# Seven block products instead of eight for batch 1's second expert layer, in a fused kernel on one Trainium2 core

## The chip, the cores and the metric

The kernel runs on one core of one Trainium2 chip. The metric is the device time of one execution in microseconds. Before the change it is 1129.08 us, the median of three runs (1128.8 to 1129.44).

## What is computed

Three stages follow each other on 2304 tokens (4 batches of 576, here columns) with 512 features. An attention over 32 memory slots gives `x`; a layer pair `x @ w_in` (512 to 2048), leaky ReLU, `@ w_out` follows; the last stage, where the change lies, mixes four experts:

```python
def _moe2_ref(x, domain_probs, w1, w2):          # x 2304x512, w1 4x512x1024, w2 4x1024x512
    p = domain_probs / (domain_probs.sum(-1, keepdims=True) + 1e-09)
    out = np.zeros((N, D), dtype=np.float32)
    for e in range(E):
        h = np.maximum(x @ w1[e], 0.0)
        out += p[:, e:e + 1] * (h @ w2[e])
    return out.astype(np.float32)
```

## The kernel before

Every float32 operand of a large product is split into a high part (a cast on ScalarE) and a low part (the difference, on VectorE or GpSimd). A product of two 128x128 by 128x288 blocks is then three matmuls: high by high, high by low, low by high (`PASSES`).

The experts' 4 x 1024 hidden features are cut into eight groups `g` of 512, and each group into two halves `hp` of 256. A *unit* is one group for one batch. The plan of `plan_experts` (L1110) runs in two halves: in the first, units (g, 0) and (g, 1) for g = 0 to 7, in the second (g, 2) and (g, 3). Within a unit, class `Up` makes the first product by Strassen's algorithm: seven block products `p1` to `p7` per half, 6 matmuls each, into three PSUM tiles (`ux`, `uy`, `uw`), from which `v1`, `v16`, `v167`, `c11`, `c22`, `c21`, `c12` form the four blocks of `h`; a gate then takes the maximum with zero and multiplies by `p`. The second product of a unit runs beside the first product of the next one, in the places that `down()` leaves.

There are two forms of the second product. Class `Down` (L981), for batches 0 and 1 and for group 7, makes 8 products of 12 matmuls (L1000), from the gated `h` split into `g` tiles. Class `Seven` (L1024), for batches 2 and 3 in groups 0 to 6, uses Strassen's algorithm: differences of gated blocks (`sum`, L1040), high and low parts into `gc` tiles, 14 products of 6 matmuls (L1060), evacuated into seven accumulators per batch (`flush`, L1075), which `combine` turns into the output at the end. Its weights are four blocks of `w2` and four operand sums `S1` to `S4`, made in the first half by `s_sum` (GpSimd), `s_part` and `s_keep`, stored in DRAM and loaded in the second half.

```python
self.seven, self.hs = b > 1 and g < NG - 1, None                     # Up, L888 on
def c11(self):
    nc.scalar.copy(out=self.block(0, 0), in_=self.x)
def c22(self):
    self.add(self.block(1, 1), self.w, self.v167_t)
def gate(self, i):
    h = self.h[:, 2 * i:2 * i + 2].rearrange("p j n -> p (j n)")
    nc.vector.scalar_tensor_tensor(out=h, in0=h, scalar=0.0, in1=p_t[self.g // 2, self.b], op0=ALU.max, op1=ALU.mult)
```

PSUM holds six banks for `ux`, `uy`, `uw` (`ps_a`) and two for the second product (`ps_h`). The pool `big` has ten buffers; in the first half seven hold the operands `x` of batches 0 and 1, and the `g` tiles share the rest. Every engine takes its instructions in order. That order is the list `ORDER` (L30) of task names, such as `p1_300` (product 1 of group 3, batch 0, half 0), `D21_3` and `F21_3` (product 3 of group 2, batch 1, and its evacuation), `H`/`L` (high, low part), `S` (difference); `ON_VECTOR` (L254) says which low parts and differences go to VectorE and not to GpSimd. Before the change the list keeps one regular order, that of the plan, from group 2 of the first half to group 4 of the second; before and behind these (groups 0 and 1, the layer pair of the second stage, and the last groups) it is irregular. The change makes it irregular from group 0 of the first half to group 1 of the second, and regular from there to group 6.

## Time and profile before

| what | value |
|---|---|
| median of three runs | 1129.08 us |
| profiled execution: its time, its span | 1128.83 us, 1126.7 us |
| TensorE busy, matmuls | 1117.2 us, 8752 |
| VectorE, ScalarE, GpSimd busy | 797.8, 440.8, 529.7 us |
| DMA moved | 181.21 MB |

The span is the time between the first and the last instruction; 2.1 us of the execution lie around it. Busy times count an engine's instructions, overlaps once; in the profile PE is TensorE's matmuls, PEld its weight loads, DVE VectorE, ACT ScalarE, POOL GpSimd, SP the queue that issues the transfers. `L1000` is a line of the kernel. A tile's name stands left of the arrow, what it is made from right of it. A matmul's duration holds the time in which the next one already runs.

### The profile page before, as it was taken

To read this page: it belongs to the slowest core of one execution; us is meant where nothing else is said; L and a number is where in the kernel's file an instruction comes from. 1 tells how busy PE (TensorE), PEld (TensorE's weight loads), DVE (VectorE), ACT (ScalarE), POOL (GpSimd) and SP (SyncE) were. 2 spreads that over 40 slices of the span, in tenths; PEclk is the share of its full clock that TensorE was granted. 3 is DMA by queue.
4 is the path that set the end of the run, shared out by engine and by line. 5 is a ranking of instruction groups with operands and counts; after the bars stand their busy time and mean duration, and the time that the engine had idled before them with its cause. 6 is when DMAs were issued, how large, how long until landed. Compare 5 with 4: busy or idle time off the path is not lost.

```text
span 1126.7 us, 22094 instructions
## 1 busy us (share of the span) xinstructions
PE 1117.2 (99%) x8752; PEld 1082.7 (96%) x8752; DVE 797.8 (71%) x1469; ACT 440.8 (39%) x916; POOL 529.7 (47%) x432
## 2 busy tenths in 40 slices
PE   9999999999999999999999999999999999999998
PEld 7679999999999999999999999999999999999998
DVE  6987787667556766576676767687577777777776
ACT  5776655544444444233333323333432222222220
POOL 3666545523346567474554745433333333334650
PEclk9999999999999999999999999999999999999999
DMA  9930212111021449373653637675556455555432
GB/s 378 394 124 20 94 57 76 57 39 40 1 86 42 152 156 355 114 293 142 241 224 132 260 147 269 233 260 183 161 180 186 160 181 159 176 163 169 134 109 87
DMA packets 64503, 181.21 MB, mean 161 GB/s; under 512 B 6672, under 2 KB 23056, under 8 KB 60688
## 3 DMA queue, kind: packets, MB, share of 16 engines
...
## 4 chain that ended last, share of the span: by engine, by line
PE 95%; DVE 2%; POOL 1%; issue 1%; DMA 0%; ACT 0%; POOLq 0%; DVEq 0%; ACTq 0%
PE o L1000 19%; PE y L688 17%; PE c L1060 13%; PE uy L887 13%; PE h L654 9%; PE uw L887 8%; PE ux L887 8%; PE y L685 1%; PE pw L613 1%; PE warm L320 1%; PE pm L422 1%; PE h L651 1%; PE pc L454 0%; POOL w L307 0%; DMA raww<-in_w 0%
## 5 line engine op out<-in xcount | busy, mean ns | idle before, releaser
L1000 PE MATMUL o<-g,w 128*128 128x288 f32 x1536 | 223.3, 295 | 1.6 <-ACT acc L1015 1.6
L1000 PEld LDWEIGHTS o<-g,w 128*128 128x128 f32 x1536 | 210.0, 188 | 1.8 <-ACT acc L1015 1.8
L688 PE MATMUL y<-g,wout 128*128 128x288 f32 x1440 | 205.3, 296 | 0.0
L688 PEld LDWEIGHTS y<-g,wout 128*128 128x128 f32 x1440 | 195.3, 188 | 7.3 <-ACT g L673 2.5
L887 PE MATMUL uy<-x,w 128*128 128x288 f32 x1152 | 184.7, 296 | 0.4 <-DVE v L921 0.4
L887 PEld LDWEIGHTS uy<-x,w 128*128 128x128 f32 x1152 | 163.1, 188 | 1.9 <-DVE v L921 1.7
L1060 PE MATMUL c<-gc,w2c 128*128 128x288 f32 x1008 | 155.9, 295 | 0.5 <-ACT acc L1073 0.5
L1060 PEld LDWEIGHTS c<-gc,w2c 128*128 128x128 f32 x1008 | 140.9, 188 | 1.0 <-ACT acc L1073 1.0
L307 POOL TENSOR_TENSOR gc<-h,gc 128x576 fp32r<-128x576 f32 x54 | 81.5, 1517 | 124.9 <-ACT gc L1047 91.5
L307 POOL TENSOR_TENSOR g<-act,g 128x288 fp32r<-128x288 f32 x78 | 67.6, 873 | 121.1 <-ACT g L673 86.3
L887 PE MATMUL uw<-x,w 128*128 128x288 f32 x768 | 122.6, 295 | 0.0
L887 PE MATMUL ux<-x,w 128*128 128x288 f32 x768 | 122.1, 295 | 0.0
L654 PE MATMUL h<-a,wp 128*128 128x288 f32 x720 | 110.2, 296 | 0.0
L887 PEld LDWEIGHTS uw<-x,w 128*128 128x128 f32 x768 | 108.8, 188 | 0.1
L887 PEld LDWEIGHTS ux<-x,w 128*128 128x128 f32 x768 | 108.8, 188 | 0.0
L669 DVE SCALAR_TENSOR_TENSOR act<-neg,bet,h 128x288 f32<-128x288 f32 x120 | 60.2, 509 | 65.2 <-ACT neg L660 59.4
L654 PEld LDWEIGHTS h<-a,wp 128*128 128x128 f32 x720 | 100.0, 188 | 5.7 <-issue 2.3
L1047 ACT CAST gc<-h 128x576 fp32r<-128x576 f32 x70 | 47.1, 675 | 146.2 <-DVE h L1040 114.8
L1017 DVE TENSOR_TENSOR acc<-o,acc 128x288 f32<-128x288 f32 x112 | 50.7, 453 | 69.5 <-PE o L1000 69.5
L307 POOL TENSOR_TENSOR w<-raww,w 128x512 fp32r<-128x512 f32 (+1 forms) x45 | 69.1, 1551 | 62.4 <-ACT w L791 38.9
L921 DVE TENSOR_TENSOR v<-uy,v 128x288 f32<-128x288 f32 x128 | 58.1, 454 | 48.5 <-PE uy L887 45.6
L660 ACT ACTIVATE neg<-h 128x288 f32<-128x288 f32 x128 | 52.2, 411 | 97.4 <-PE h L654 94.9
(175 smaller groups left out, 1627.3 us busy)
## 6 DMA issues: line engine op xcount, KB each, us to landing
...
```

The lines of the kernel that those rows point to most:

```text
L307: eng.tensor_tensor(out=out, in0=in0, in1=in1.bitcast(F32), op=ALU.subtract)
L320: mm(p[:, 0:128], ident, ident, start=True, stop=True)
L654: mm(p, wp_t[b, c, g][:, x, fs], a_t[b][:, y, g, o:o + HB], start=(n == 0), stop=(n == 5))
L660: nc.scalar.activation(out=self.neg, in_=self.p, func=AF.Relu, scale=-1.0)
L669: nc.vector.scalar_tensor_tensor(out=self.g, in0=self.neg, scalar=bet[:, ft:ft + 1], in1=self.p, op0=ALU.mult, op1=ALU.add)
L688: mm(First.acc[d], w[:, x, d * 128:(d + 1) * 128], self.gt[:, y, 0:HB], start=(self.start and n == 0), stop=(self.stop and n == 2))
L887: mm(p, w[:, x, a, k], operand(self.b, i)[:, y, k], start=(start and n == 0), stop=(n == 5), skip_group_check=not start)
L921: nc.vector.tensor_tensor(out=out, in0=x, in1=y, op=ALU.add)
L1000: mm(p, w[:, x, i, d % 2 * 128:(d % 2 + 1) * 128], g, start=(m == 0), stop=(m == 11), skip_group_check=len(hps) == 1)
L1017: nc.vector.tensor_tensor(out=a, in0=self.ps[n], in1=a, op=ALU.add)
L1047: nc.scalar.copy(out=t[:, 0], in_=self.raw(q))
L1060: mm(p, w[:, x, i, m * 128:(m + 1) * 128], self.g_t[q][:, y, i], start=(k == 0), stop=(k == 5))
```

## The change

`Up.seven` becomes true for batch 1 too (groups 0 to 6), so that its second product is a `Seven`. It takes the blocks of `w2` and the sums `S1` to `S4` from the slots of the weight pool, into which `s_hi` and `s_lo` now write the sums' parts directly; a sum is stored by one transfer of 512 KB where there were two of 256 KB. For batches 0 and 1 (`banked`) the additions `c22`, `c21`, `c12` write back into PSUM, and each block is gated from there into `h`; `c11` is a gate in place of a copy by ScalarE. Batch 1's accumulators are combined during group 7 of the first half. Three pools grow, the reserve for dynamic DMA shrinks, and `ORDER` and `ON_VECTOR` are rewritten.

```diff
...
-F20_6 p3_211 c12_211 ws31 D20_7 F20_7 p1_300 p6_300 v1_300 hi1_211 gate0_211 hi0_211 v16_300 lo1_211 lo0_211 p5_300
+S21_4 p1_300 F20_7 H21_3 L21_3 wk30 F21_0 wh31 wl310 D21_3 D21_2 rw27 vh311 v1_300 p2_300 F21_3 H21_2 H21_4 wl311
...
     def to_experts():
...
-        for name, key, bufs in (("w1b", ("w1", 1), 1), ("pp", "p", 2), ("hp", "h", 2), ("vp", "v", 1), ("ring2", "w2", 6), ("accp", "acc", 2), ("yt", "y", 4), ("xt", "xt", 2)):
+        for name, key, bufs in (("w1b", ("w1", 1), 1), ("pp", "p", 2), ("hp", "h", 3), ("vp", "v", 1), ("ring2", "w2", 8), ("accp", "acc", 2), ("yt", "y", 6), ("xt", "xt", 2)):
...
-        t = pools["xt"].tile([128, 2, HB], F32, tag="xt", name=f"{n}{g}").rearrange("p k n -> p (k n)")[:, 0:512]
-        cs_t[g, n] = [t]
-        x, y = (cs_t[g, i][0] if i in ("S1", "S2") else a[i] for i in (x, y))
-        nc.gpsimd.tensor_tensor(out=t, in0=x, in1=y, op=op)
...
-    def s_part(g, n, part):
...
-        t = pools["y"].tile([128, 2, HB], F32R, tag="y", name=f"{n}{g}{part}").rearrange("p k n -> p (k n)")[:, 0:512]
-        src = cs_t[g, n]
-        src.append(t)
-        if part == 0:
-            nc.scalar.copy(out=t, in_=src[0])
-        else:
-            sub_to(nc.vector, t, src[0], src[1])
...
-    def s_keep(g, n, part):
-        if ("w2", g, n) not in kept_t:
-            kept_t["w2", g, n] = dram.tile([128, 2, 512], F32, name=f"k{n}{g}")
-        nc.sync.dma_start(out=kept_t["w2", g, n][:, part], in_=cs_t[g, n][1 + part].bitcast(F32))
+        o = cs_t[g, n] = pools["xt"].tile([128, 2, HB], F32, tag="xt", name=f"{n}{g}").rearrange("p k n -> p (k n)")[:, 0:512]
+        x, y = (cs_t[g, i] if i in ("S1", "S2") else a[i] for i in (x, y))
+        nc.gpsimd.tensor_tensor(out=o, in0=x, in1=y, op=op)
...
+    def s_hi(g, n):
+        t = kept_t["w2", g, n] = c_ops[g, (P5, P6, P3, P7)[("S1", "S2", "S4", "S3").index(n)]] = pools["w2"].tile([128, 2, 512], F32R, tag="w", name=f"s{n}{g}")
+        nc.scalar.copy(out=t[:, 0], in_=cs_t[g, n])
...
+    def s_lo(g, n):
+        t = kept_t["w2", g, n]
+        sub_to(engine(f"sl{g}{n}"), t[:, 1], cs_t[g, n], t[:, 0])
...
+    def s_keep(g, n):
+        kept_t["w2", g, n] = keep(kept_t["w2", g, n], f"k{n}{g}")
...
+    def b_late(b):
+        return b > 1
...
         def __init__(self, g, b, hp):
...
-            self.seven, self.hs = b > 1 and g < NG - 1, None
+            self.seven, self.hs = b > 0 and g < NG - 1, None
+            self.banked = b < 2
...
         def open(self):
...
-            if self.seven and self.hp:
+            if self.seven and self.hp and b_late(self.b):
...
         def c11(self):
-            nc.scalar.copy(out=self.block(0, 0), in_=self.x)
+            if self.banked:
+                self.gated(0, 0, self.x)
+            else:
+                nc.scalar.copy(out=self.block(0, 0), in_=self.x)
...
+        def gated(self, i, j, src):
+            p = p_t[self.g // 2, self.b][:, j * HB:(j + 1) * HB]
+            nc.vector.scalar_tensor_tensor(out=self.block(i, j), in0=src, scalar=0.0, in1=p, op0=ALU.max, op1=ALU.mult)
...
+        def added(self, i, j, bank, x, y):
+            if self.banked:
+                self.add(bank, x, y)
+                self.gated(i, j, bank)
+            else:
+                self.add(self.block(i, j), x, y)
...
         def c22(self):
-            self.add(self.block(1, 1), self.w, self.v167_t)
+            self.added(1, 1, self.x, self.w, self.v167_t)
...
         def c21(self):
-            self.add(self.block(1, 0), self.y, self.v1_t)
+            self.added(1, 0, self.y, self.y, self.v1_t)
...
         def c12(self):
-            self.add(self.block(0, 1), self.w, self.v16_t)
+            self.added(0, 1, self.w, self.w, self.v16_t)
...
         def flush(self, n):
...
-            if b > 1:
+            if b > 0:
...
         def __init__(self, g, b, n, ups):
...
-            self.ps, self.slot = {}, {q: max(7 * n + k, 0) % 6 for q, k in ((P1, -1), (P5, 1), (P2, 2), (P3, 3), (P7, 4), (P6, 5), (P4, 7))}
+            self.ps, self.late, self.pairs = {}, b_late(b), {}
+            self.slot = {q: max(7 * n + k, 0) % 6 for q, k in ((P1, -1), (P5, 1), (P2, 2), (P3, 3), (P7, 4), (P6, 5), (P4, 7))}
+            if not self.late:
+                self.slot = {P1: 0, P5: 1, P2: 2, P3: 3, P7: 4, P6: 5, P4: 2}
...
         def hi(self, q):
...
-            if k // 2 not in c_slot:
-                c_slot[k // 2] = unit(f"gc{k // 2}", F32R).rearrange("p (s x i n) -> p s x i n", s=2, x=2, i=2)
-            t = self.g_t[q] = c_slot[k // 2][:, k % 2]
+            c = c_slot if self.late else self.pairs
+            if k // 2 not in c:
+                c[k // 2] = unit(f"gc{self.name}{k // 2}", F32R).rearrange("p (s x i n) -> p s x i n", s=2, x=2, i=2)
+            t = self.g_t[q] = c[k // 2][:, k % 2]
...
         def product(self, n):
...
-            w = c_ops[self.g, q].rearrange("p x (i n) -> p x i n", i=2)
+            if not self.late and q in (P1, P2, P4):
+                w = w2_t[(self.g,) + C_W[q]]
+            else:
+                w = c_ops[self.g, q]
+            w = w.rearrange("p x (i n) -> p x i n", i=2)
...
-                for key, c in (("y", 3),) if b == 2 else (("y", 1), ("xt", 2)):
+                for key, c in (("y", 1), ("xt", 2)) if b == 3 else (("y", 3),):
...
+                if b == 1:
+                    l = acc_t[b]
+                    acc_t[b] = [l[k] for k in (4, 0, 1, 2, 5, 6, 3)]
...
         def do_part(g, n, part):
-            do(f"sq{g}{n}{part}", s_part, g, n, part)
-            do(f"sk{g}{n}{part}", s_keep, g, n, part)
+            if part:
+                do(f"sl{g}{n}", s_lo, g, n)
+                do(f"sk{g}{n}", s_keep, g, n)
+            else:
+                do(f"sh{g}{n}", s_hi, g, n)
...
+            if (half, g, t) == (0, NG - 1, 1):
+                for n, place in enumerate(((0, 0), (0, 0), (0, 1), (0, 1), (0, 2), (0, 2), (0, 3))):
+                    more.setdefault(place, []).append((do_combine, 1, n))
...
-                more.setdefault((0, 2), []).extend((do_unspill, 2, i, j) for i in range(2) for j in range(2))
+                more.setdefault((0, 2), []).extend((do_unspill, 2, i, j) for i, j in ((0, 0), (0, 1), (1, 1)))
...
+                        parts.insert(0, ((0, 0), [(do_unspill, 2, 1, 0)]))
...
-                n_seven += 1
+                n_seven += b > 1
+                c.defer = not old_seven
...
-                    h_do(last, "gate", 0)
-                    h_do(last, "hi", 0)
+                    if not last.banked:
+                        h_do(last, "gate", 0)
+                    if (half, g, t, hp) != (1, NG - 1, 0, 1):
+                        h_do(last, "hi", 0)
...
-                    h_do(last, "gate_half", 1)
+                    if not last.banked:
+                        h_do(last, "gate_half", 1)
...
+                        if old.defer:
+                            s_do(old, f"H{P2}", f"L{P2}")
...
-                    h_do(last, "lo", 0)
+                    if (half, g, t, hp) != (1, NG - 1, 0, 1):
+                        h_do(last, "lo", 0)
...
+                if (half, g, t, hp) == (1, NG - 1, 0, 1):
+                    for i in (1, 0):
+                        h_do(last, "hi", i)
+                        h_do(last, "lo", i)
...
-                    h_do(u, "gate_half", 0)
+                    if not u.banked:
+                        h_do(u, "gate_half", 0)
...
-                    else:
+                    elif not c.defer:
...
-                    h_do(u, "gate", 1)
+                    if not u.banked:
+                        h_do(u, "gate", 1)
...
-                        h_do(u, "hi", 1)
-                        h_do(u, "lo", 1)
+                        if (half, g, t) != (1, NG - 1, 0):
+                            h_do(u, "hi", 1)
+                            h_do(u, "lo", 1)
...
-    nc = bacc.Bacc("TRN2", target_bir_lowering=False, num_devices=1)
+    nc = bacc.Bacc("TRN2", target_bir_lowering=False, num_devices=1, dynamic_dma_scratch_size=1024)
...
```

Three places show how the instructions move. On TensorE, at the start of unit (3, 0), the second product of unit (2, 1) runs beside the first product; `o210` was its output block 0, `c213` is its block product 3. Before:

```order
L887 MATMUL ux300_6631<-x00_4267,w130_6508 128x288 x6
L887 MATMUL uy300_6638<-x00_4267,w130_6508 128x288 x6
L887 MATMUL uw300_6655<-x03_4382,w130_6508 128x288 x6
L887 MATMUL ux300_6631<-x03_4382,w130_6508 128x288 x6
L887 MATMUL uy300_6638<-x04_4680,w130_6508 128x288 x6
L1000 MATMUL o210_6686<-g210_6441,w2200_6248 128x288 x6
L1000 MATMUL o210_6686<-g211_6647,w2210_6253 128x288 x6
L887 MATMUL uy300_6638<-x04_4680,w130_6508 128x288 x6
L1000 MATMUL o211_6711<-g210_6441,w2200_6248 128x288 x6
L1000 MATMUL o211_6711<-g211_6647,w2210_6253 128x288 x6
```

Now:

```order
L888 MATMUL ux300_6644<-x00_4267,w130_6520 128x288 x6
L1083 MATMUL c213_6662<-gc210_6439,sS12_6206 128x288 x6
L1083 MATMUL c212_6669<-gc210_6439,sS12_6206 128x288 x6
L888 MATMUL ux300_6644<-x03_4382,w130_6520 128x288 x6
L888 MATMUL uy300_6697<-x00_4267,w130_6520 128x288 x6
L1083 MATMUL c211_6706<-gc210_6439,w2200_6149 128x288 x6
L888 MATMUL uw300_6714<-x03_4382,w130_6520 128x288 x6
L1083 MATMUL c216_6727<-gc211_6652,sS42_6634 128x288 x6
L888 MATMUL uy300_6697<-x04_4680,w130_6520 128x288 x6
L888 MATMUL uy301_6745<-x00_4267,w131_6658 128x288 x6
L1083 MATMUL c218_6752<-gc212_6690,sS32_6571 128x288 x6
L1083 MATMUL c214_6759<-gc211_6652,w2210_6388 128x288 x6
```

Groups of 12 matmuls for one output (two rows each) have become groups of 6, out of their numerical order, and three of them (`c218`, `c214`, `c215`) follow each other.

On VectorE, in unit (3, 1), half 0. Before:

```order
L921 TENSOR_TENSOR v16310_6928<-uy310_6915,v1310_6922 128x288
L307 TENSOR_TENSOR g301_6924<-h301_6794,g301_6924 128x576 x2
L921 TENSOR_TENSOR v167310_6973<-uy310_6915,v1310_6922 128x288
L921 TENSOR_TENSOR h310_6961<-uw310_6948,v167310_6973 128x288
L307 TENSOR_TENSOR S431_6976<-S43_6892,S430_6963 128x512
L1017 TENSOR_TENSOR acc0_5292<-o300_6983,acc0_5292 128x288
L921 TENSOR_TENSOR h310_6961<-uy310_6915,v1310_6922 128x288
L970 SCALAR_TENSOR_TENSOR h310_6961<-h310_6961,p11_6091 128x576
L1017 TENSOR_TENSOR acc0_5292<-o301_7013,acc0_5292 128x288
L921 TENSOR_TENSOR h310_6961<-uw310_6948,v16310_6928 128x288
```

Now:

```order
L922 TENSOR_TENSOR v16310_6947<-uy310_6931,v1310_6939 128x288
L952 SCALAR_TENSOR_TENSOR h310_6949<-ux310_6862,p11_5915 128x288
L922 TENSOR_TENSOR v167310_6963<-uy310_6931,v1310_6939 128x288
L922 TENSOR_TENSOR ux310_6862<-uw310_6974,v167310_6963 128x288
L952 SCALAR_TENSOR_TENSOR h310_6949<-ux310_6862,p11_5915 128x288
L922 TENSOR_TENSOR uy310_6931<-uy310_6931,v1310_6939 128x288
L952 SCALAR_TENSOR_TENSOR h310_6949<-uy310_6931,p11_5915 128x288
L309 TENSOR_TENSOR g301_6966<-h301_6878,g301_6966 128x576
L922 TENSOR_TENSOR uw310_6974<-uw310_6974,v16310_6947 128x288
L952 SCALAR_TENSOR_TENSOR h310_6949<-uw310_6974,p11_5915 128x288
```

Additions wrote `h` and a gate of 576 columns followed; now they write their PSUM tile, and a gate of 288 columns reads it.

On GpSimd, from unit (2, 1) into (3, 0). Before, from the last sums of `w1` on:

```order
L782 TENSOR_TENSOR s31_6612<-raww17_6380,s31_6612 128x256
L307 TENSOR_TENSOR w131_6670<-raww17_6380,w131_6670 128x768
L307 TENSOR_TENSOR g300_6708<-h300_6668,g300_6708 128x576 x2
L307 TENSOR_TENSOR w2300_6810<-raww26_6556,w2300_6810 128x512
L307 TENSOR_TENSOR w2310_6815<-raww27_6684,w2310_6815 128x512
L826 TENSOR_TENSOR S13_6820<-raww26_6556,raww27_6684 128x512
L826 TENSOR_TENSOR S23_6835<-S13_6820,raww26_6556 128x512
L826 TENSOR_TENSOR S43_6892<-raww27_6684,S23_6835 128x512
L826 TENSOR_TENSOR S33_6932<-raww26_6556 128x512
L307 TENSOR_TENSOR w2301_6934<-raww26_6556,w2301_6934 128x512
L307 TENSOR_TENSOR w2311_6939<-raww27_6684,w2311_6939 128x512
L307 TENSOR_TENSOR g310_7005<-h310_6961,g310_7005 128x576
```

Now:

```order
L309 TENSOR_TENSOR gc210_6439<-h210_6404,gc210_6439 128x576
L827 TENSOR_TENSOR S42_6575<-raww25_6116,S22_6259 128x512
L784 TENSOR_TENSOR s31_6588<-raww17_6586 128x256
L784 TENSOR_TENSOR s31_6588<-s31_6588,raww17_6586 128x256
L784 TENSOR_TENSOR s31_6588<-raww17_6586 128x256
L784 TENSOR_TENSOR s31_6588<-raww17_6586,s31_6588 128x256
L309 TENSOR_TENSOR gc211_6652<-h211_6485,gc211_6652 128x576
L309 TENSOR_TENSOR sS42_6634<-S42_6575,sS42_6634 128x512
L1058 TENSOR_TENSOR h210_6404<-h211_6485,h210_6404 128x576
L827 TENSOR_TENSOR S13_6723<-raww26_6721,raww27_6676 128x512
L309 TENSOR_TENSOR gc212_6690<-h210_6404,gc212_6690 128x576
L1058 TENSOR_TENSOR h210_6404<-h210_6404,h211_6485 128x576
```

Low parts (`gc`) and differences (`h210`) of the block products and low parts of operand sums (`sS42`) stand among the work on weights.

## Rows read from the trace of the kernel before

**Rows 1.** The page's head: span, and busy time of each engine.
```profile
span 1126.7 us, 22094 instructions
...
PE 1117.2 (99%) x8752; PEld 1082.7 (96%) x8752; DVE 797.8 (71%) x1469; ACT 440.8 (39%) x916; POOL 529.7 (47%) x432
```

**Rows 2.** Stretches of the span, busy us (instructions) of each engine, granted clock, DMA.
```profile
core 0: us, PE busy (x) PEld busy (x) DVE busy (x) ACT busy (x) POOL busy (x), PEclk, DMA share, GB/s
75.00:375.00 300.00, 300.00 (x2372) 286.16 (x2365) 207.68 (x400) 153.09 (x355) 142.38 (x139) 1.00 0.15 51
375.00:450.00 75.00, 73.40 (x552) 73.05 (x551) 50.19 (x74) 32.55 (x65) 51.80 (x38) 1.00 0.67 245
450.00:725.00 275.00, 275.00 (x2068) 274.18 (x2068) 186.12 (x307) 89.46 (x156) 153.01 (x124) 1.00 0.53 203
725.00:825.00 100.00, 99.05 (x741) 98.10 (x740) 70.83 (x114) 41.26 (x85) 32.88 (x21) 1.00 0.65 205
825.00:1050.00 225.00, 225.00 (x1699) 224.94 (x1698) 167.16 (x337) 61.15 (x111) 81.11 (x55) 1.00 0.54 170
1010.00:1100.00 90.00, 89.57 (x672) 89.21 (x671) 65.82 (x124) 21.95 (x42) 46.09 (x30) 1.00 0.40 131
```

**Rows 3.** The chain that ended last, shares of the span by engine.
```profile
PE 95%; DVE 2%; POOL 1%; issue 1%; DMA 0%; ACT 0%; POOLq 0%; DVEq 0%; ACTq 0%
```

**Rows 4.** What TensorE waited for: us in total, times, longest.
```profile
PE o L1000 <- ACT acc L1015: 1.6, 1, 1.6
```

**Rows 5.** The chain in order of time: start us, us, what.
```profile
847.20 1.59 PE c L1060 x12
...
1106.01 17.50 PE o L1000 x132
```

**Rows 6.** Groups of VectorE, 425 to 750 us: busy us, mean ns | idle before.
```profile
L970 DVE SCALAR_TENSOR_TENSOR h<-h,p 128x576 f32<-128x576 f32 x56 | 58.0, 1036 | 3.4 <-ACT h L944 2.4
...
L1017 DVE TENSOR_TENSOR acc<-o,acc 128x288 f32<-128x288 f32 x104 | 47.1, 453 | 67.5 <-PE o L1000 67.5
...
L307 DVE TENSOR_TENSOR S<-S,S 128x512 fp32r<-128x512 f32 x24 | 24.9, 1039 | 1.3 <-ACT acc L1015 0.6 <-ACT S L834 0.2
...
L307 DVE TENSOR_TENSOR w<-s,w 128x1024 fp32r<-128x1024 f32 x12 | 19.6, 1631 | 2.1 <-ACT w L791 2.1
```

**Rows 7.** Groups of GpSimd, 425 to 750 us.
```profile
L307 POOL TENSOR_TENSOR g<-h,g 128x576 fp32r<-128x576 f32 x29 | 42.0, 1450 | 42.5 <-ACT g L976 41.1 <-DMA raww<-in_w 1.4
...
L307 POOL TENSOR_TENSOR w<-raww,w 128x512 fp32r<-128x512 f32 x28 | 39.4, 1427 | 23.2 <-ACT w L861 23.2
...
L307 POOL TENSOR_TENSOR w<-raww,w 128x768 fp32r<-128x768 f32 x12 | 22.3, 1858 | 38.9 <-ACT w L791 38.9
```

**Rows 8.** Groups of GpSimd, VectorE and ScalarE in the second half, 825 to 1050 us.
```profile
L307 POOL TENSOR_TENSOR gc<-h,gc 128x576 fp32r<-128x576 f32 x40 | 60.2, 1514 | 102.1 <-ACT gc L1047 71.9 <-issue 30.2
...
L1040 DVE TENSOR_TENSOR h<-h 128x576 f32<-128x576 f32 x10 | 7.5, 748 | 0.0
...
L1047 ACT CAST gc<-h 128x576 fp32r<-128x576 f32 x50 | 33.7, 675 | 118.7 <-DVE h L1040 109.7 <-DVE h L953 5.0 <-POOL h L1040 4.0
```

**Rows 9.** Three groups of the whole span, shapes apart.
```profile
L669 DVE SCALAR_TENSOR_TENSOR act<-neg,bet,h 128x288 f32<-128x288 f32 x120 | 60.2, 509 | 65.2 <-ACT neg L660 59.4 <-POOL g L307 3.8 <-POOL mout L587 1.3
...
L307 DVE TENSOR_TENSOR w<-raww,w 128x768 fp32r<-128x768 f32 x3 | 3.1, 1033 | 0.7 <-ACT w L791 0.7
...
L307 POOL TENSOR_TENSOR w<-s,w 128x1024 fp32r<-128x1024 f32 x2 | 4.8, 2409 | 4.3 <-ACT w L791 4.3
```

**Rows 10.** Timeline, 520 to 570 us, of VectorE, then GpSimd: start us, us, what.
```profile
533.00 0.45 DVE L1017 TENSOR_TENSOR acc<-o,acc 128x288 f32<-128x288 f32 x1
...
533.37 1.76 DVE L970 SCALAR_TENSOR_TENSOR h<-h,p 128x576 f32<-128x576 f32 x1
...
539.55 0.76 DVE L970 SCALAR_TENSOR_TENSOR h<-h,p 128x576 f32<-128x576 f32 x1
...
533.22 1.29 POOL L826 TENSOR_TENSOR S<-raww 128x512 f32<-128x512 f32 x1 [0.69 <-PE ux L887]
```

352 lines of the change are left out of this document (177 added, 175 removed).

## Prediction

> **What bounds the kernel now.** I read the page's first parts, then the stretches, then what TensorE waits for, and last the prices of single instructions. TensorE is busy for 1117.2 of 1126.7 us [rows 1], and the chain that ended last is 95% TensorE [rows 3]. Busy alone would not prove it, since a matmul's end is modelled; so look at the stretches [rows 2]. From 450 to 725 us, where the first half of the experts runs, TensorE is busy for 275.00 of 275.00 us, while VectorE has 186 us of work, ScalarE 89 and GpSimd 153. The second half (825 to 1050 us), where batches 2 and 3 already use the seven products that batch 1 is now to get, is just as full: 225.00 of 225.00 us. The idle time of TensorE in the expert phase lies at the seams: 1.60 us behind one ScalarE evacuation between 375 and 450 us, and 0.95 us between 725 and 825 us [rows 2, 4]. So here time falls one for one with the matmuls, as long as the others keep up.
>
> The price of a matmul is not the duration that a profile gives it, since matmuls overlap. What counts is the pitch. [...]
>
> **What the change removes from TensorE.** For each of groups 0 to 6 batch 1's second product goes from 8 products of 12 matmuls (96) to 14 of 6 (84). That is 7 x 12 = 84 matmuls fewer, and nothing else on TensorE changes in number. 84 x 132.6 ns = 11.14 us. A pair of units (batches 0 and 1 of a group) falls from 360 matmuls, 47.7 us, to 348, 46.1 us.
>
> **What it adds elsewhere, per pair, counted in group 3.**
> VectorE has 32.3 us of work in 47.7 now (186.12/275). The 8 gates of 576 columns at 1036 ns become 16 of 288 that read PSUM. The trace of before has no such gate; the same operation with one PSUM source takes 509 ns [rows 9], a plain addition from PSUM 453 ns [rows 6], and the far end is the whole price of the wide gate, 1036. I take 509, the nearest: 8.14 instead of 8.29 us. The 12 additions that now write back into PSUM have no row either: 453 ns as when they write SBUF, with 1036 as the far end again and nothing below, since no row of this width is shorter. At both far ends VectorE would gain 12 x 0.58 + 16 x 0.53 = 15.4 us and be the bound, with 48.1 us per pair; I don't expect it, because both PSUM-reading rows of this width lie at 453 and 509 ns. The accumulations go from 16 to 22 (6 x 0.453 = +2.7 us), the four low parts of operand sums leave for GpSimd (4 x 1.039 = -4.2), two 768-wide low parts come (2 x 1.033 = +2.1), one 1024-wide goes (-1.6), two differences of gated blocks come (2 x 0.748 = +1.5) [rows 6, 8, 9]; low parts of activations stay at four. Sum +0.4: 32.7 us of 46.1, 71%.
>
> GpSimd has 26.6 us per pair now (153.01/275). Low parts of activations go from 4 x 1.450 to 2 x 1.450 and 4 x 1.514 (+3.2), operand sums add 3 x 1.427 (+4.3), a 768-wide part leaves (-1.9), a 1024-wide comes (+2.4), two block differences come, priced as the low parts of that width (2 x 1.514 = +3.0) [rows 7 to 9]. That is +11.0, so 37.6 us of 46.1: from 56% to 82%. This is the engine to watch.
>
> ScalarE loses four evacuations of 288 per pair and gains three casts of 576; at 33% busy [rows 2] this is covered. SP issues 28 stores of 512 KB in place of 56 of 256 KB: the same bytes in fewer issues, and DMA holds 0% of the chain [rows 3]. The seven combining steps of batch 1 run once, beside group 7's products, at about 0.75 us on VectorE and 1.5 on GpSimd each [rows 8]: hidden there. The larger pools (three activation tiles, eight weight slots, six small tiles) only take waits away. The smaller reserve for dynamic DMA I cost at nothing: it could only slow transfers, which hold 0% of the chain. The second half keeps its instructions, and its 225.00 us without a gap is the cover if some of them change engine.
>
> **Where waits can come in.** PSUM has two banks for these products. Now a product lasts 12 matmuls, 1.59 us, and an evacuation has that long; with 6 matmuls it has 0.80 us when two of them stand together, and in the new order three do (products 8, 4 and 5 of group 2): the evacuation, 0.45 us, then has some 0.3 us of slack, and a low part of some 0.75 us [rows 8] stands ahead of it on VectorE. And a VectorE instruction that works from SBUF alone can be held up: the gate (L970) that starts at 533.37 us takes 1.76 us while a GpSimd subtraction runs from 533.22, the one at 539.55 takes 0.76 with GpSimd idle, and additions from PSUM take 0.45 either way [rows 6, 10]. The gates leave that exposed form; low parts and differences stay in it, beside a busier GpSimd.
>
> How much is lost so I take from stretches of the present kernel whose order is irregular, as the first half's now becomes. In the expert stage 375 to 450 and 1010 to 1100 us hold 1.60 and 0.43 us of idle TensorE, 2.03 in 165 us or 1.23 per 100; the irregular layer pair (75 to 375 us) holds none [rows 2]. For the 350 us of the first half that bounds the new idle time by 0 and 4.3 us. The present idle time of the part that is reordered, 1.60 + 0.95 = 2.55 us, goes in exchange. The net lies between -2.55 and +1.75; I take +1.0, near the upper end because GpSimd is fuller than in any of these stretches.
>
> **Sum.** The profiled execution took 1128.83 us, 0.25 below the median of three runs. 1128.83 - 11.14 + 1.0 = 1118.7 us.
>
> **The rivals.**
> *The seams close as well.* No new wait, and the 2.55 us go: 1128.83 - 11.14 - 2.55 = 1115.1 us. For it: 75 to 375 us runs without a gap in an irregular order, and the pools have grown. Against: the three products in a row.
>
> *GpSimd falls behind and the kernel gets slower.* GpSimd takes its instructions in order and now waits 47.7 - 26.6 = 21.1 us per pair, mostly for ScalarE's casts [rows 7]. With 37.6 us of work, 8.5 us of waiting fit into 46.1. If half of the present waiting stays (10.6 us), a pair takes 48.2 us: 7 x (48.2 - 46.1) = 14.7 us more than 1117.7, so 1132.4 us, slower. It decides at 10.1 us of waiting, where a pair is as long as now. TensorE would then wait for low parts on GpSimd. Against it: several low parts are issued long before their product. Half-way cases (1 us per pair, 7 us in all) give 1125.7 us with the forecast's other terms. [...]
>
> *The saving doesn't arrive.* The operand buffers decide it: ten, of which seven hold the inputs of batches 0 and 1, so three are left, and the second product of batch 1 wants three beside batch 0's two. The operand of the third product can be written only when batch 0's last product has run; cast (0.68) and low part (1.51 on GpSimd) [rows 8] then stand before it, with about eight groups of 6 matmuls, 6.4 us, as cover. If GpSimd is over 4 us behind there, some 1.6 us per pair are lost: 1128.8 us, no change.
>
> **Chances.** Forecast 0.60, seams closed 0.15, half-way 0.12, slower through GpSimd 0.07, saving lost 0.06. A measurement of this kernel can tell about 0.2%, 2.3 us, from no change. Faster: 0.60 + 0.15 + 0.12 = 0.87; same 0.06; slower 0.07. The range reaches from the closed seams to the half-way cases and leaves out the last two: 1115.0 to 1126.5 us.
>
> **What would show it.** Right: 84 matmuls fewer at the same pitch; 25.00 of 25 us busy through most of the first half; pairs of 46.1 us; gates from PSUM near 0.5 us; GpSimd near 80% there. Wrong: waits of TensorE for low parts or blocks on GpSimd (POOL) in every pair, a pitch above 133 ns, PSUM gates near 1 us, or a new gap of several us at a seam.

## The result and the profile after

The changed kernel takes 1115.3 us (median; 1115.18 to 1115.43), the kernel before on the same chip 1129.09 us: a ratio of 0.9878, 95% interval 0.9861 to 0.9895. That is 13.8 us less. The forecast was 1118.7 us; the time lies inside the range (1115.0 to 1126.5), 3.4 us below the forecast, and all but on the rival of the closed seams (1115.1). The profiled execution took 1115.43 us, with a span of 1113.3.

The page's head and the chain by engine of the changed kernel [rows 1, 3]:

```profile
span 1113.3 us, 21930 instructions
...
PE 1105.6 (99%) x8668; PEld 1071.8 (96%) x8668; DVE 806.9 (72%) x1570; ACT 443.6 (40%) x911; POOL 605.0 (54%) x487
...
PE 97%; DVE 2%; issue 0%; ACT 0%; POOL 0%; POOLq 0%; DVEq 0%
```

8668 matmuls are 84 fewer than 8752. GpSimd has 75 us more work, VectorE 9. The stretches show where that lies [rows 2]; the columns are as there:

```profile
375.00:450.00 75.00, 74.77 (x560) 74.21 (x560) 54.22 (x91) 35.47 (x70) 61.02 (x47) 1.00 0.54 201
450.00:725.00 275.00, 274.64 (x2061) 273.68 (x2060) 209.08 (x407) 96.09 (x160) 223.81 (x171) 1.00 0.58 217
725.00:825.00 100.00, 100.00 (x756) 100.00 (x756) 60.04 (x110) 37.58 (x79) 50.37 (x34) 1.00 0.65 221
825.00:1050.00 225.00, 225.00 (x1699) 224.94 (x1698) 168.61 (x339) 62.74 (x113) 87.00 (x58) 1.00 0.53 176
```

TensorE idles for 0.23 us from 375 to 450 us (1.60 before), for 0.36 from 450 to 725 (none before) and not at all from 725 to 825 (0.95 before). GpSimd's work in the stretch from 450 to 725 rose from 153.01 to 223.81 us, 81% of it. The 132 matmuls at the end of the chain keep their pitch, 17.52 / 132 = 132.7 ns [rows 5]:

```profile
1092.60 17.52 PE o L1015 x132
```

What the weight loads of TensorE wait for from 375 us on adds up to 5.2 us in the kernel before (first) and to 2.5 us in the changed one (the columns: us in total, times, longest; four and five lines in all, of which two and three stand here):

```profile
PEld o L1000 <- ACT acc L1015: 1.8, 1, 1.8
PEld uy L887 <- DVE v L921: 1.7, 7, 0.5
...
```
```profile
PEld c L1083 <- DVE acc2y L1101: 0.8, 1, 0.8
PEld c L1083 <- DVE acc L1101: 0.6, 1, 0.6
...
PEld c L1083 <- DVE gc L309: 0.2, 1, 0.2
```

The spans differ by 13.4 us, of which 84 x 132.6 ns = 11.14 are matmuls; the other 2.3 us are about what the waits have lost (5.2 - 2.5 = 2.7). Groups of VectorE, then of GpSimd, from 450 to 725 us [rows 6 to 9]:

```profile
L952 DVE SCALAR_TENSOR_TENSOR h<-ux,p 128x288 f32<-128x288 f32 x48 | 21.8, 454 | 8.2 <-PE ux L888 7.0 <-issue 0.3
...
L309 DVE TENSOR_TENSOR gc<-h,gc 128x576 fp32r<-128x576 f32 x17 | 16.5, 972 | 2.0 <-ACT gc L1066 2.0
...
L922 DVE TENSOR_TENSOR ux<-uw,v 128x288 f32<-128x288 f32 x24 | 11.1, 464 | 3.6 <-PE uw L888 3.1
...
L309 DVE TENSOR_TENSOR g<-h,g 128x576 fp32r<-128x576 f32 x9 | 10.5, 1164 | 0.1
```
```profile
L309 POOL TENSOR_TENSOR gc<-h,gc 128x576 fp32r<-128x576 f32 x23 | 35.2, 1532 | 12.0 <-ACT gc L1066 12.0
...
L309 POOL TENSOR_TENSOR g<-h,g 128x576 fp32r<-128x576 f32 x15 | 21.9, 1467 | 9.0 <-ACT g L991 9.0
```

A gate that reads PSUM takes 454 ns, an addition that writes back into PSUM 464. VectorE's low parts, which work from SBUF alone, take 0.97 and 1.16 us.

### The profile page after: what moved, and what is told of

It is laid out like the page before. It is cut to its first block, busy times and chain, and to the rows that moved or that the text cites. A ratio compares the mean times of both kernels' runs of the same rounds, so it can differ in the third digit from the quotient of the medians.

```text
span 1113.3 us, 21930 instructions
## 1 busy us (share of the span) xinstructions
PE 1105.6 (99%) x8668; PEld 1071.8 (96%) x8668; DVE 806.9 (72%) x1570; ACT 443.6 (40%) x911; POOL 605.0 (54%) x487
## 4 chain that ended last, share of the span: by engine, by line
PE 97%; DVE 2%; issue 0%; ACT 0%; POOL 0%; POOLq 0%; DVEq 0%
PE c L1083 20%; PE y L690 17%; PE uy L888 14%; PE o L1015 13%; PE uw L888 9%; PE ux L888 9%; PE h L656 9%; PE y L687 1%; PE pw L615 1%; PE warm L322 1%; PE pm L424 1%; PE h L653 1%; PE pc L456 0%; DVE w L309 0%; DVE h L1058 0%
## 5 line engine op out<-in xcount | busy, mean ns | idle before, releaser
L309 POOL TENSOR_TENSOR gc<-h,gc 128x576 fp32r<-128x576 f32 x78 | 117.6, 1514 | 119.5 <-ACT gc L1066 119.4
L1066 ACT CAST gc<-h 128x576 fp32r<-128x576 f32 x119 | 79.3, 675 | 196.6 <-DVE h L1058 121.5
L1015 PE MATMUL o<-g,w 128*128 128x288 f32 x864 | 122.4, 295 | 0.0
L1015 PEld LDWEIGHTS o<-g,w 128*128 128x128 f32 x864 | 117.1, 188 | 0.0
L1101 DVE TENSOR_TENSOR acc<-c,acc 128x288 f32<-128x288 f32 x144 | 64.9, 454 | 35.4 <-PE c L1083 33.3
L922 DVE TENSOR_TENSOR v<-uy,v 128x288 f32<-128x288 f32 x128 | 58.1, 454 | 40.2 <-PE uy L888 36.9
L675 ACT CAST g<-act 128x288 fp32r<-128x288 f32 x120 | 51.2, 433 | 43.7 <-DVE act L671 32.9
```

Source lines behind the costliest of these rows:

```text
L309: eng.tensor_tensor(out=out, in0=in0, in1=in1.bitcast(F32), op=ALU.subtract)
L675: nc.scalar.copy(out=self.gt[:, 0, 0:HB], in_=self.g)
L922: nc.vector.tensor_tensor(out=out, in0=x, in1=y, op=ALU.add)
L1015: mm(p, w[:, x, i, d % 2 * 128:(d % 2 + 1) * 128], g, start=(m == 0), stop=(m == 11), skip_group_check=len(hps) == 1)
L1066: nc.scalar.copy(out=t[:, 0], in_=self.raw(q))
L1101: nc.vector.tensor_tensor(out=a, in0=self.ps[n], in1=a, op=ALU.add)
```

## The experiments

The theory after the result: TensorE is the bound before and after, a matmul removed is worth its pitch, and it arrives here because the gates out of PSUM, the written order and the dealing of engines keep VectorE's and GpSimd's work out of TensorE's way. Its rivals: the time comes from the seams, the larger pools or the gates by themselves and not from the matmuls; or the matmuls bring it whatever stands around them. Four questions follow: is the saving the matmuls, which part of the change makes it possible, how near is GpSimd to its limit, and is there anything left. All times are medians, each with its ratio to the kernel before on the same chip.

### Is the saving the matmuls?

**The 84 matmuls put back.** One of batch 1's seven products is issued twice; its second pass writes the same result over the first.

```diff
-            k = 0
-            for i in range(2):
+            for again in range(2 if not self.late and q == P4 else 1):
+                k = 0
+                for i in range(2):
```

> The changed kernel, with the 6 matmuls of batch 1's fourth block product issued twice in groups 0 to 6 (2 outputs x 6 x 7 = 84 matmuls put back; the second set overwrites the first, so the output stays the reference's). Theory A (the time follows the number of matmuls, and about 2.4 us came from waits at seams that the new order no longer has): 1115.3 + 84 x 0.1326 = 1126.4 us, between 1126 and 1127.5, still 2 to 3 us under the kernel before. Rival B (order, pools and lighter VectorE gates made the gain, the count did not matter): 1115 to 1118 us.

Measured: 1127.22 us (1126.1 to 1129.41), ratio 0.9984 (0.9975 to 0.9993); TensorE has 8752 matmuls again and is busy for 448.58 of the 450 us from 375 to 825 us (449.41 in the changed kernel). That is 11.9 us over the changed kernel for 84 matmuls: 11.14 at the pitch, and one new wait of 0.8 us. The wait is TensorE's for VectorE's `v` (L922), and the time lies within theory A's bounds. All the other parts of the change are still there, so the bulk of the saving is count times pitch.

**The seams mended in the kernel before.** Four pieces of batch 1's weights come later in `ORDER`, and seven differences leave the table of VectorE (of that table this diff, as the ones below, shows the names that leave or come, not the whole lines); nothing else.

```diff
-rw22 ss1S1 vh100 vl100 wl110 wk11 p4_100 c11_100 c21_100 vk100 p1_101 F01_2 D01_1
+rw22 wl110 wk11 p4_100 c11_100 c21_100 p1_101 F01_2 ss1S1 vh100 vl100 vk100 D01_1
...
-x2t0 x2t1 x2t2 x2t3 x3t0 x3t1 x3t3
```

> The kernel before, without any of the change, but with its two worst seams mended in the order: ScalarE evacuates product 2 of group 0 ahead of a cast that waits for a weight transfer, and the seven differences for the operands of batches 2 and 3 go to GpSimd. Theory A: the 1.75 us at 425 us and 0.39 us each at 730 and 754 us go, so 1.6 to 2.6 us less than before: 1126.5 to 1127.5 us, with no change in the matmuls. Rival B (the idle time only moves to the next wait): 1129 us. What is missing between this and the 2.4 us must then lie in the second half.

Measured: 1128.0 us (1127.43 to 1130.39), ratio 0.9993 (0.9984 to 1.0001), span 1125.7 against 1126.7. The wait of 1.6 us behind ScalarE [rows 4] is gone, but a new one stands right behind its place:

```profile
PE ux L887 <- ACT v L925: 1.0, 1, 1.0
```

That lies between theory A and rival B: about 1 us of the 2.55 can be had by such a mending, and the seam partly moves. The interval reaches to no change.

### Which part makes it possible?

**The gates alone.** The kernel before with its direct product for batch 1, the blocks of batches 0 and 1 gated out of PSUM; `gate` does nothing for them. One load of gates, and the second product or the corner of five units, come a few places earlier, as the new order of writing needs.

```diff
         def c11(self):
-            nc.scalar.copy(out=self.block(0, 0), in_=self.x)
+            if self.banked:
+                self.gated(0, 0, self.x)
+            else:
+                nc.scalar.copy(out=self.block(0, 0), in_=self.x)
...
-            self.add(self.block(1, 1), self.w, self.v167_t)
+            self.added(1, 1, self.x, self.w, self.v167_t)
...
         def gate(self, i):
+            if self.banked:
+                return
```

> The kernel before, batch 1 still as a direct second product in the first half, with the PSUM gates alone (each block of batches 0 and 1 gated out of its bank, and the gates of 576 columns in SBUF gone; one load of gates, the corner p2/c11 of five pairs and nothing else come earlier in the order, as the new place of c11 needs). Together with the run whose gates stay in SBUF it fills the square of the two parts. Theory A (the gates bought nothing on TensorE's path by themselves: before, their waits are under 2 us in all; they are worth something only where Strassen's operand sums fill VectorE and GpSimd): 1129.1, within 1127.8 to 1129.9, so the 14 us of the other run are a product of both parts together. Rival B (the gates help by themselves, so part of the change's gain is theirs): under 1127. Rival C (the c11 block is now VectorE's and no longer ScalarE's, and the two ops of the other blocks sit in the banks' way: slower without Strassen): above 1130.5.

Measured: 1127.37 us (1126.5 to 1129.67) against 1128.8, ratio 0.9989 (0.998 to 0.9998): 1.4 us less, between theory A and rival B, with an interval that only just leaves out no change. The idle time from 375 to 450 us falls from 1.60 [rows 2] to 0.25, and the wait behind the accumulation of ScalarE is not there:

```profile
375.00:450.00 75.00, 74.75 (x563) 74.45 (x562) 48.54 (x89) 30.81 (x59) 48.86 (x40) 1.00 0.67 247
450.00:725.00 275.00, 275.00 (x2075) 275.00 (x2074) 175.79 (x355) 80.16 (x136) 144.93 (x122) 1.00 0.55 208
725.00:825.00 100.00, 98.62 (x736) 97.44 (x735) 69.91 (x117) 38.44 (x80) 32.98 (x21) 1.00 0.60 194
```

ScalarE's timeline, of the kernel before and then of this run, has the place:

```profile
424.08 0.62 ACT L861 CAST w<-raww 128x512 fp32r<-128x512 f32 x1 [4.93 <-DMA raww<-in_w]
424.60 0.39 ACT L944 COPY h<-ux 128x288 f32<-128x288 f32 x1
424.89 0.40 ACT L1015 COPY acc<-o 128x288 f32<-128x288 f32 x1
```
```profile
422.42 0.62 ACT L861 CAST w<-raww 128x512 fp32r<-128x512 f32 x1 [2.65 <-DMA raww<-in_w]
422.94 0.39 ACT L1032 COPY acc<-o 128x288 f32<-128x288 f32 x1
```

In the kernel before, the copy of a corner (L944) stands between a cast that waited 4.93 us for a load and the evacuation that TensorE waits for; here the corner is VectorE's. The load also comes 1.7 us earlier, so how much of the 1.35 us each of the two is worth was not tried apart.

**Strassen without the gates.** The changed kernel, but three of the four blocks of batches 0 and 1 are added into SBUF and gated there, in place.

```diff
-                self.add(bank, x, y)
-                self.gated(i, j, bank)
+                self.add(self.block(i, j), x, y)
+                self.gated(i, j, self.block(i, j))
```

> The changed kernel, with the additions of c22, c21 and c12 written to SBUF and their gates of 288 columns read from there (12 of 16 gates per pair), everything else as it is. Theory A (a VectorE instruction from SBUF alone is held up while GpSimd works, and VectorE has idle time to take it): the mean of these gates rises from 0.46 us to 0.65 to 0.9, VectorE's busy time in 450 to 725 us rises by 12 to 30 us, TensorE loses a few evacuations: 1115.5 to 1120 us. Rival B (a gate of 288 columns is too short to be held up, and PSUM brings nothing): mean 0.46 us, 1115.3 us. Rival C (gating from PSUM is what makes the saving possible): over 1122 us.

Measured: 1129.31 us (1128.33 to 1131.43), ratio 1.0005 (0.9996 to 1.0014). The whole saving is gone, 14 us: rival C. Theory A was right on the gates and on VectorE's work (below), and wrong on what TensorE loses by it. The 84 matmuls are still missing (8668), so this is the case "the saving doesn't arrive", by a way that the prediction had not named. The stretches:

```profile
375.00:450.00 75.00, 72.10 (x534) 70.87 (x534) 61.19 (x88) 34.43 (x68) 57.89 (x42) 1.00 0.56 207
450.00:725.00 275.00, 269.15 (x1989) 264.56 (x1988) 227.59 (x391) 96.05 (x158) 225.79 (x168) 1.00 0.56 210
```

TensorE idles for 2.9 and 5.85 us there (0.23 and 0.36 in the changed kernel), its weight loads for 4.1 and 10.4 (0.8 and 1.3), so 12.5 us more together, most of the 14. (The profiled execution took 1131.43 us, at a mean granted clock of 0.998; its first gate out of PSUM starts at 381.6 us, in the changed kernel at 379.0.) The largest of TensorE's waits is for VectorE, which has 18.5 us more work in the second stretch. That wait, the group of the gates in that stretch, and the timeline around two of them, of VectorE and then of GpSimd:

```profile
PE uy L888 <- DVE v L922: 4.6, 6, 1.4
```
```profile
L952 DVE SCALAR_TENSOR_TENSOR h<-h,p 128x288 f32<-128x288 f32 x68 | 56.9, 837 | 2.3
```
```profile
555.58 1.57 DVE L952 SCALAR_TENSOR_TENSOR h<-h,p 128x288 f32<-128x288 f32 x1
557.07 0.45 DVE L922 TENSOR_TENSOR h<-uy,v 128x288 f32<-128x288 f32 x1
557.55 0.46 DVE L952 SCALAR_TENSOR_TENSOR h<-h,p 128x288 f32<-128x288 f32 x1
```
```profile
555.54 1.29 POOL L309 TENSOR_TENSOR sS<-S,sS 128x512 fp32r<-128x512 f32 x1
557.74 2.56 POOL L309 TENSOR_TENSOR w<-s,w 128x1024 fp32r<-128x1024 f32 x1 [0.91 <-ACT w L793]
```

The first gate starts 0.04 us behind a GpSimd instruction and ends 0.32 us behind its end; the second starts in GpSimd's pause and takes 0.46; the addition between them reads PSUM and takes 0.45. All instructions of the gates' line, duration in ns as least, median and most, in this run and then in the changed kernel:

```profile
L952 DVE SCALAR_TENSOR_TENSOR h<-h,p x96: 457/810/1632, 383.0 to 750.1; 128x288 f32<-128x288 f32 x96
```
```profile
L952 DVE SCALAR_TENSOR_TENSOR h<-ux,p x64: 440/458/462, 379.0 to 729.3; 128x288 f32<-128x288 f32 x64
```

Out of PSUM all 128 gates of the changed kernel take 440 to 462 ns (the 64 of the other two banks lie within these bounds), with GpSimd at 81%: 110 of them start beside a GpSimd instruction, 18 in a pause of it. The 32 of this run that still read PSUM take 440 to 460. Three more of this run's gates out of SBUF, at 525.58, 527.31 and 553.68 us, start beside a GpSimd instruction; they take 1.33, 1.06 and 0.74 us and end 0.31 to 0.32 us behind its end. One at 524.34 us starts in a pause and takes 0.46. What holds such a gate until then was not shown. The order of the work was made for gates out of PSUM; whether another order would carry SBUF gates was not tried.

The four kernels make a square:

| batch 1's second product | gates of batches 0, 1 | us | kernel before, same chip |
|---|---|---|---|
| direct | SBUF, 576 columns | 1129.09 | the same kernel |
| direct | PSUM | 1127.37 | 1128.8 |
| seven products, new order | SBUF, 288 columns, three blocks of four | 1129.31 | 1129.13 |
| seven products, new order | PSUM | 1115.3 | 1129.09 |

The gates alone are worth 1.4 us, the seven products alone (with their order, pools and dealing of engines) nothing, both together 13.8.

**The larger pools alone**, in the kernel before.

```diff
-        for name, key, bufs in (("w1b", ("w1", 1), 1), ("pp", "p", 2), ("hp", "h", 2), ("vp", "v", 1), ("ring2", "w2", 6), ("accp", "acc", 2), ("yt", "y", 4), ("xt", "xt", 2)):
+        for name, key, bufs in (("w1b", ("w1", 1), 1), ("pp", "p", 2), ("hp", "h", 3), ("vp", "v", 1), ("ring2", "w2", 8), ("accp", "acc", 2), ("yt", "y", 6), ("xt", "xt", 2)):
...
-    nc = bacc.Bacc("TRN2", target_bir_lowering=False, num_devices=1)
+    nc = bacc.Bacc("TRN2", target_bir_lowering=False, num_devices=1, dynamic_dma_scratch_size=1024)
```

> The kernel before, with only the larger pools (3 activation tiles, 8 weight slots, 6 small tiles) and the smaller reserve for dynamic DMA. Theory A: the seams wait for a queue, not for a buffer, so 1129 us, within 0.5. Rival B (more buffers close the seams): 1126 to 1127.5 us.

Measured: 1128.75 us (1128.27 to 1129.66), ratio 0.9997 (0.9988 to 1.0007). That is theory A: by themselves they do nothing, and the smaller reserve costs nothing. That the new order needs them was not tried.

**The planner's order.** The changed kernel with the planner's regular sequence in place of the written one from the third group's first product to batch 2's, engines as in the table.

```diff
-        for name in ORDER.split():
-            run(name)
+        names = ORDER.split()
+        i = names.index("p1_200")
+        planned = [name for name, fn, args in plan]
+        for name in names[:i] + planned[:planned.index("p1_220")] + names[i:]:
+            if name in tasks:
+                run(name)
```

> The changed kernel, with the planner's regular order in place of the written one from group 2 of the first half to group 1 of the second. 84 matmuls fewer stay. Theory A (the order is worth what its waits cost, a few us): 1116 to 1122 us. Rival B (without the new order the saving is lost, because the regular one puts GpSimd's work in the wrong places): 1126 us or more.

Measured: 1168.84 us (1168.04 to 1171.27), ratio 1.0355 (1.034 to 1.0371): 53.5 us over the changed kernel, 40 over the one before: rival B. What TensorE waits for, and the stretches (the last three of 5 us each):

```profile
PE c L1083 <- POOL gc L309: 13.8, 5, 3.9
PE c L1083 <- DVE acc L1101: 13.4, 11, 2.7
```
```profile
450.00:725.00 275.00, 249.17 (x1790) 245.73 (x1789) 177.26 (x350) 84.05 (x139) 185.84 (x149) 0.96 0.51 191
725.00:825.00 100.00, 87.64 (x629) 85.92 (x628) 65.34 (x112) 29.41 (x54) 62.54 (x43) 0.95 0.57 198
...
765.00:770.00 5.00, 0.00 (x0) 0.00 (x0) 0.00 (x0) 0.00 (x0) 5.00 (x5) 0.87 0.69 218
770.00:775.00 5.00, 1.94 (x8) 1.95 (x9) 3.66 (x7) 1.77 (x3) 2.29 (x3) 0.50 0.11 38
775.00:780.00 5.00, 5.00 (x26) 5.00 (x25) 1.01 (x3) 2.84 (x6) 5.00 (x4) 0.61 0.53 170
```

25.8 and 12.4 us of idle time make 38. A good part of the rest is the clock: TensorE stood still from 765 to 770 us, and in the next five it was granted 0.50 (8 matmuls in 1.94 busy us, 243 ns each); from 775 to 780 us it ran 26 matmuls in 5.00 us, where 38 fit at the pitch. From 450 to 825 us nine stretches of 5 us have matmuls at a clock below 0.9; what they lack against the pitch is some 74 matmuls, an estimate of 10 us.

**The same with engines dealt by a rule**, since the table was made for the other order: in groups 2 to 6 all of batch 1's low parts and differences on VectorE, low parts of batch 0 and of the weights on GpSimd (35 names leave the table of VectorE, 40 come).

```diff
-lo0_300 lo0_500 lo1_200 lo1_211 lo1_301 lo1_311 lo1_401 lo1_411 lo1_500 lo1_511 lo1_611
...
-wl201 wl210 wl211 wl310 wl311 wl400 wl401 wl410 wl500 wl510 wl511 wl601 wl610 wl611 wl700 wl701 wl710
+L21_1 L21_3 L21_5 L21_6 S21_5 S21_6
...
```

> The planner's regular order again in the stretch of the second product, but with the engines dealt by a rule instead of the table made for the written order: in groups 2 to 6 all of batch 1's low parts and operand differences on VectorE, the low parts of batch 0's h and of the weights on GpSimd. The run with the written table lost 53 us. Theory A (the order itself costs it: evacuations and operand work come late whatever engine does them): at least +30 us over the changed kernel, 1145 or more. Rival B (the loss was a table that did not fit the order): under 1130. Between the two, each holds in part; the waits say which: A evacuations late on VectorE (acc, o, c), B GpSimd's gc.

Measured: 1151.81 us (1151.23 to 1153.72), ratio 1.0204 (1.019 to 1.0218): theory A for the most part. The 13.8 us behind GpSimd's `gc` are gone, half of them now behind VectorE's, and with it 17 of the 53.5 us; the evacuations of VectorE are late still:

```profile
PE o L1015 <- DVE acc L1032: 8.3, 1, 8.3
PE c L1083 <- DVE gc L309: 6.9, 6, 1.3
PE c L1083 <- DVE acc L1101: 6.2, 11, 1.6
```

So a third of that loss was the table, and two thirds (36.5 us) stay with the order under this dealing; other dealings were not tried, nor was an order made by another rule. The wait of 8.3 us for the evacuation of line 1032, which both runs have, may come of the place where the planned piece is joined to the written one; it was not taken out.

### How near is GpSimd to its limit?

**Nine low parts of batch 0's activations from VectorE to GpSimd**, in the changed kernel: nine names leave VectorE's table. (It is a line shorter, so line numbers stand one lower.)

```diff
-lo0_001 lo0_300 lo0_500 lo1_000 lo1_100 lo1_200 lo1_301 lo1_401 lo1_500
```

> The changed kernel, with the nine low parts of batch 0's activations (groups 0 to 6) that VectorE makes given to GpSimd. GpSimd's busy time in 450 to 725 us goes from 223.8 to about 237 of 275 us (86%). Theory A (GpSimd has slack until its work and its waits fill the pair): under 1 us longer, 1115.3 to 1116.3 us. Rival B (it is already at its limit): each part costs its 1.47 us, 13 us more, 1128 us.

Measured: 1123.53 us (1122.25 to 1125.18), ratio 0.9951 (0.9937 to 0.9966): 8.2 us more than the changed kernel. Nine such parts at 1.467 us are 13.2 us of work on GpSimd; over half of it arrives at the end. Between A and B, since A's bound for what fits was too wide:

```profile
PE o L1014 <- POOL g L308: 5.0, 4, 1.8
```
```profile
450.00:725.00 275.00, 271.05 (x2009) 269.77 (x2008) 200.31 (x391) 96.32 (x159) 223.10 (x172) 0.99 0.56 211
```

GpSimd is not busier by share (223.10 of 275 us, 81%, where 86% was expected) although it has more to do, because the kernel waits for it. Not all of the 8.2 us are waits. The granted clock is 0.99 in that stretch, and behind the longest wait the matmuls come slower:

```profile
538.18 3.36 PE L1014 MATMUL o<-g,w 128*128 128x288 f32 x17 [1.81 <-POOL g L308]
541.34 1.64 PE L887 MATMUL uy<-x,w 128*128 128x288 f32 x6
542.78 1.03 PE L887 MATMUL ux<-x,w 128*128 128x288 f32 x6
```

From start to start the 17 take 3.16 us and the next six 1.44, 186 and 240 ns each where the pitch is 132.7. At this one place that is an estimate of 1.5 us. The order stayed the one written for the other dealing; whether another order has room for these parts was not tried.

**Also 21 low parts of operand sums.**

```diff
-L01_2 L01_3 L01_4 L11_0 L11_4 L21_0 L21_2 L21_4 L31_2 L31_3 L31_4
-L41_0 L41_1 L41_2 L51_0 L51_2 L51_3 L61_0 L61_1 L61_4 L61_5
```

> As the run before, with the 21 low parts of batch 1's operands that VectorE makes given to GpSimd too: some 263 of 275 us (96%). Theory A: the 11 to 12 us of waiting per pair that GpSimd has left no longer fit, TensorE waits for low parts in every pair, and the time rises by 5 to 40 us: 1120 to 1155 us; a first half that is as long as GpSimd's queue. Rival B (low parts are always early enough, GpSimd never decides): under 1117 us.

Measured: 1145.24 us (1144.46 to 1146.41), ratio 1.0144 (1.0129 to 1.0159), 30 us over the changed kernel and 16 over the one before: theory A, and the slower case of the rivals exists: TensorE waits 11.0 us for `gc` and 5.9 us for `g` parts on GpSimd. GpSimd's share is 85%, where 96% was expected, since the waits stretch the time in which it works.

```profile
PE c L1081 <- POOL gc L307: 11.0, 5, 5.5
```
```profile
450.00:725.00 275.00, 260.74 (x1898) 257.93 (x1899) 174.68 (x347) 90.68 (x150) 233.13 (x184) 0.98 0.51 192
```

### What is left?

In the changed kernel the gap at 705 us lies behind an evacuation that stands behind a low part of 1.84 us beside a GpSimd instruction:

```profile
701.86 2.54 POOL L309 TENSOR_TENSOR w<-raww,w 128x512 fp32r<-128x512 f32 x2 [1.23 <-ACT w L858]
...
703.18 1.84 DVE L309 TENSOR_TENSOR g<-h,g 128x576 fp32r<-128x576 f32 x1
...
704.94 0.81 DVE L1101 TENSOR_TENSOR acc<-c,acc 128x288 f32<-128x288 f32 x2
705.44 0.83 PEld L1083 LDWEIGHTS c<-gc,sS 128*128 128x128 f32 x6 [0.59 <-DVE acc L1101]
```

**Two pieces moved.**

```diff
-v16_701 lo0_700 D61_5 vl701 sl6S2 x2t1 vl710 p5_701 D61_4 F61_5
+v16_701 D61_5 vl701 sl6S2 x2t1 vl710 p5_701 D61_4 F61_5 lo0_700
...
-gate_half1_631 S63_5 H63_3 wr715 D62_12 F62_12 F62_7
+F62_7 gate_half1_631 S63_5 H63_3 wr715 D62_12 F62_12
```

> The changed kernel, with its two largest remaining gaps mended: at 705 us an evacuation goes ahead of a low part that GpSimd holds up for 1.84 us, at 1051 us another ahead of a difference held up for 2.03 us. Theory A: 0.53 and 0.69 us less, 1114.1 us, between 1113.9 and 1114.8. Rival B (the next wait takes their place): 1115.3 us.

Measured: 1114.65 us (1113.99 to 1115.54), ratio 0.9872 (0.9856 to 0.9889), span 1112.8; the median lies within theory A's bounds, the highest run above rival B's value. The gap at 705 us is gone, the one at 1051 remains: the difference `S63_5` still takes 2.03 us beside GpSimd with the evacuation behind it.

**Three pieces moved**: one more than in the run above, against which the diff stands; the changed kernel ran once more beside it.

```diff
-F62_7 gate_half1_631 S63_5 H63_3 wr715 D62_12 F62_12
+F62_7 gate_half1_631 H63_3 wr715 D62_12 F62_12 S63_5
```

> The changed kernel once more, as the yardstick for the next run on the same chip: 1115.0 to 1115.7. Both theories expect the same of it; a value outside would put the earlier differences of under 1 us in doubt.

> The changed kernel with three pieces moved: the two of the earlier mended version (the low part lo0_700 behind the evacuation F61_5, and F62_7 ahead of gate_half1_631) and, new, the difference S63_5 behind the evacuation F62_12, whose 2.03 us beside a GpSimd operation held the bank at 1051 us. Theory A (what idles on TensorE at these two seams is order alone): the gaps at 705 and 1051 us are both gone, together 1.0 to 1.4 us off, 1114.0 to 1114.6. Rival B (the seam moves: what now runs beside the GpSimd operation is the next thing late, or TensorE is at its pitch and the end is set elsewhere): 1114.7 to 1115.6.

Measured: the changed kernel 1115.04 us (1114.94 to 1115.26), ratio 0.9875 (0.9862 to 0.9889), span 1113.3 again; the mended one 1114.61 us (1113.75 to 1115.22), ratio 0.9872 (0.9857 to 0.9887), span 1112.1. In its profile the gap at 705 us is gone and of the 0.54 us at 1051 some 0.19 are left, behind the next evacuations; the evacuation that was held now runs ahead of the difference, which takes 1.29 us:

```profile
1049.55 0.46 DVE L1101 TENSOR_TENSOR acc2y<-c,acc2y 128x288 f32<-128x288 f32 x1 [0.48 <-PE c L1083]
...
1049.93 1.29 DVE L1058 TENSOR_TENSOR h<-c,h 128x576 f32<-128x576 f32 x1
```

0.4 us off the median, at the border of theory A and rival B, and 1.2 off the span, while the spreads of the runs overlap: both mended versions beat the kernel before by 1.3%, and that they beat the changed one is not shown.

## Why the prediction was right, and where its steps were not

**The removal.** Right. The pitch of 132.6 ns is 17.50 us over 132 matmuls [rows 5], at a granted clock of 1.00 [rows 2]; a single matmul's duration is 295 ns in the mean. 84 x 132.6 ns = 11.14 us; putting the matmuls back cost 11.9 with a wait of 0.8 in it, and the pitch after is 132.7 ns.

**The new waits, +1.0 us.** Mis-sized, and of the wrong sign: by the spans the waits fell by 2.3 us, near the lower bound of -2.55. The step that failed is the choice of a value near the upper end "because GpSimd is fuller than in any of these stretches". A fuller GpSimd alone was no sign of idle time on TensorE: with 223.81 us of work in 275 it left 0.36. The seams closed, as the first rival had it. One of them, at 425 us, had closed with the gates alone (1.35 of its 1.60 us); the 0.95 us from 725 to 825 closed only in the whole change (the gates alone left 1.38 there, the pools alone 1.06), and by which part of it was not tried. The prediction gave this case 0.15: the time lies in the range, but at its edge.

**The gates.** Right in kind, wrong in weight. 509 ns was taken; measured are 454 to 458, like a plain addition. The additions into PSUM cost 460 to 464 against 453 forecast. But the sum booked the gates as 8.14 for 8.29 us and their leaving the exposed form as a remark, which no term of the sum held. That remark carries the change: with the gates in SBUF they take 837 ns in the mean, and the 14 us are gone.

**VectorE per pair.** 32.7 us forecast, 209.08 x 46.1 / 275 = 35.0 measured, although the gates came cheaper. The low parts were priced at what they took beside GpSimd at 56%. The low part of a 576-wide activation is the plain case, in the run with the gates alone:

```profile
L307 DVE TENSOR_TENSOR g<-h,g 128x576 fp32r<-128x576 f32 x24 | 17.0, 750 | 0.0
```

There GpSimd works 144.93 of 275 us and the part takes 750 ns; in the changed kernel, beside 223.81, the same part takes 1164, and the `gc` parts of that size 972. The 26 of them are 7.5 us longer than at 750 ns, by this estimate 1.3 of the 2.3 us per pair. The low part that was to stand ahead of an evacuation had been taken at 0.75 us, too, from a row of differences.

**GpSimd per pair.** 37.6 us forecast, 223.81 x 46.1 / 275 = 37.5 measured. The agreement is in part luck, since two terms (counted in group 3) miss in opposite directions: the block differences take 28.5 us in the stretch, 4.8 per pair against 3.0 forecast, the low parts of operand sums 3.1 against 4.3. The 51.2 us of pause are 8.6 per pair, 29.6 of the 51.2 behind ScalarE. That they match the rival's 8.5 us of waiting that fit shows nothing by itself: it is what a pair of 46.1 us leaves beside 37.5 of work. How near the rival was, the runs with more work say: nine more low parts on GpSimd take back 8.2 of the 13.8 us, 30 make the kernel slower than before. So, in this order of the work, it was nearer than its chance of 0.07 says.

**The operand buffers.** Cover as reckoned: ScalarE's casts into `gc` (L1066) wait six times for a matmul of batch 0's product, 12.8 us from 450 to 725, and still TensorE's only wait for a `gc` operand from 375 us on is 0.2 us.

**The pools, ScalarE, the second half.** At nothing, as forecast: the pools alone measure nothing, ScalarE rises to 35% from 450 to 725 us, the second half is busy for 225.00 of 225.00 us.

**The order.** The prediction asked what the written order would cost, 0 to 4.3 us of new idle time; TensorE idles for 0.6 us from 375 to 825. It didn't ask what that order is worth: the planner's order in its place costs 36.5 to 53.5 us.
